# Top-k attention with a SwiGLU block on one core: K and Q through three rotating buffers, transposed one turn earlier, and exp moved to the head of the turn

## The chip, the cores and the metric

The kernel runs on one core of a Trainium2 chip, as one launch. The metric is the device time of that launch in microseconds (us); the kernel before takes 1888.62 us, the median of three runs that lie between 1886.95 and 1888.98 us. One more execution was taken with the hardware profiler; its span, from the first instruction to the last, is 1884.9 us.

The engines are named as the profile names them: PE is TensorE (its matmuls), PEld its weight loads, DVE is VectorE, ACT is ScalarE, POOL is GpSimd and SP is SyncE, which here only starts transfers. Each works through its own instructions in the order in which the program gives them.

## The reference, cut to what matters

Eight batches of eight heads, 576 positions, head size 64. Each query row keeps its 32 highest scores, takes the softmax of those, and weighs V. The result, 4608 rows of 512, goes through a SwiGLU block with 1536 hidden columns. All in float32.

```
scores = (q @ k.T) / sqrt(64)                       # 8 x 8 x 576 x 576
kth    = 32nd highest of each row
scores = where(scores >= kth, scores, -1e9)
attn   = exp(scores - max);  attn /= sum(attn) + 1e-9
x      = (attn @ v), heads side by side             # 4608 x 512
g      = x @ w_gate;  val = x @ w_val               # 512 x 1536 each
out    = (g * sigmoid(g) * val) @ w_out             # 1536 x 512
```

## The kernel before

**Units and turns.** Attention is cut into 160 units: batch b (8), query tile qt (5), pair of heads hp (4). 576 queries are four tiles of 128 rows and a rest of 64. A unit with qt = 0 to 3 has two heads of 128 rows ("two halves", 2 x 576 columns); in a unit with qt = 4 the two heads' last 64 rows lie on the two halves of the partitions, so that it has one stretch of 576 columns and half of the work on DVE. A turn n of the main loop holds DVE's selection for unit n (four rounds of MAX8 and MATCH_REPLACE, then a mask), and round it the other stages of units before and after it. So each batch has sixteen full turns and then four short ones. "The border" below means these four short turns and the turn that follows them, where one batch hands over to the next.

```
for n in range(NU + 4):                              # NU = 160
    nxt   = scores([n + 1, n + 2]) if n % 2 == 1 ...  # PE, ACT copies scores to sc
    ahead = fetch(n + 3)                             # transposes of K and Q, if that unit has qt == 0
    ...
    penalize(n - 1)                                  # POOL: e = mask + sc
    flush(on_pool); flush(on_act)                    # feed-forward work put off
    if n % 2 == 1 and n >= 5:
        finish_units([n - 5, n - 4])                 # PE: attn @ v, ACT copies to xT
    run(nxt)
    dve(2)                                           # DVE: steps of unit n's selection
    ...
    pieces(2); flush(on_act)                         # PE: feed-forward matmuls
    run(turn(n - 3))                                 # PE transposes e, ACT copies to et
    weigh(n - 1)                                     # ACT: exp of e, with the row sums
    dve(1); dve(1)
    run(norm)                                        # normalize(n - 2): DVE 1/sum, ACT e *= 1/sum
    next(ahead); pieces(1); run(ahead)
    dve(1); pieces(1); dve(2); run(topk); pieces(6)
```
(cut)

**Feed-forward work is handed out by credit.** `pieces(k)` issues up to k pieces (mostly four matmuls of 128x256) while `credit` lasts; each turn adds `share(n)`, which counts how much other PE work the turn has. What is left over at the end runs after the attention.

```
def share(n):
    others = 0.6
    if n % 2 == 1:
        for m in (n - 5, n - 4, n + 1, n + 2):
            if m >= 0:
                others += 0.3 if units[m][1] == J else 0.6
    if units[n + 3][1] == 0:
        others += 0.6
    beside = 6.4 if T[1] else 7.0
    return beside * n_heads(units[n][1]) / 2 - others
```

**K and Q.** For each of the 32 pairs of heads (batch, hp), `load` brings K and Q as one tile and their last 64 rows as another; `prep` turns them on PE and ACT copies them to a slab `kqT` (and the last keys to `klast`). From the second batch on, all pairs share one buffer of each kind.

```
kq      = ld.tile([P, 2, J, 2, D], ..., name="kq_in")      # ld: bufs=1
kq_last = ld.tile([P, 2, D], ..., name="kq_last")
for n, src in ((0, k), (1, q)):                            # four large and two small transfers on SP
    ...

def prep(i):
    for n, at in ((0, 0), (None, JP), (1, S)):             # K, last rows, Q
        ps = ps_t.tile([P, 512], FP32, tag="t")            # PSUM, 5 buffers shared by all attention stages
        ... PE transposes ...
        ... ACT copies to slab (last rows: also to klast) ...

def fetch(n):
    if qt == 0:
        yield from prep(i)
        if NHP <= i + 1 < len(pairs):
            load(i + 1)
```

**V.** `load_v` brings V as `vt` and V's last 64 rows twice: as `v_last` (64 rows, both heads beside each other) for the units with qt = 4, and as `vlast`, a 128x128 tile with one head in each diagonal block, for all others.

Of the kernel before, what the change touches and what calls it, by code (L numbers as in the profile page):

```python
# [11 lines left out]
FP32 = mybir.dt.float32  # L12
# [4 lines left out]
P = 128  # L17
# [11 lines left out]
def kernel(  # L29
# [57 lines left out]
    ld = ctx.enter_context(tc.tile_pool(name="ld", bufs=1))  # L87
    slabs = ctx.enter_context(tc.tile_pool(name="slabs", bufs=4))
# [3 lines left out]
    ffn = ctx.enter_context(tc.tile_pool(name="ffn", bufs=2))  # L92
# [134 lines left out]
    raw, preps = {}, {}  # L227
    HALVES = [slice(0, D), slice(D, P)]

    def load(i):  # L230
        b, hp = pairs[i]
        h = slice(2 * hp, 2 * hp + 2)

        if 1 <= i < NHP:
            kq = ffn.tile([P, 2, J, 2, D], FP32, tag="xT", name="kq_in", bufs=3)
            kq_last = ffn.tile([P, 4, 2, D], FP32, tag="h", name="kq_last", bufs=MS + 1)[:, 0]
        else:
            kq = ld.tile([P, 2, J, 2, D], FP32, tag="kq", name="kq_in")
            kq_last = ld.tile([P, 2, D], FP32, tag="kql", name="kq_last")[:]
        for n, src in ((0, k), (1, q)):  # L240
            for hh in range(2):
                queue = nc.scalar if hh == 1 and i == 0 else nc.sync
                queue.dma_start(  # L243
                    kq[:, n, :, hh, :],
                    src[b, 2 * hp + hh, 0:JP].rearrange("(p j) d -> p j d", j=J),
                )
            nc.sync.dma_start(
                kq_last[n * R : (n + 1) * R], src[b, h, JP:S].rearrange("h p d -> p h d")
            )
        raw[i] = (kq, kq_last)  # L250

    vs = {}

    def load_v(i):
        b, hp = pairs[i]
        h = slice(2 * hp, 2 * hp + 2)
        vt = slabs.tile([P, 2, J, D], FP32, tag="v", name="v")
        v_last = slabs.tile([R, 2, D], FP32, tag="vl", name="v_last")
        vl = vlast[hp]
        nc.sync.dma_start(  # L260
            vt[:].rearrange("p h j d -> p h (j d)"),
            v[b, h, 0:JP].rearrange("h (p j) d -> p h (j d)", j=J),
        )
        nc.sync.dma_start(v_last[:], v[b, h, JP:S].rearrange("h p d -> p h d"))
        for hh in range(2):
            o = hh * R
            nc.sync.dma_start(vl[o : o + R, o : o + R], v[b, 2 * hp + hh, JP:S])
        vs[i] = (vt, v_last, vl)

    def prep(i):  # L270

        kq, kq_last = raw.pop(i)
        slab = slabs.tile([P, JP + S], FP32, tag="kqT", name="kqT")
        for n, at in ((0, 0), (None, JP), (1, S)):
            ps = ps_t.tile([P, 512], FP32, tag="t", name="kqps")
            if n is None:
                nc.tensor.transpose(
                    ps[:, 0:P], kq_last.rearrange("p h d -> p (h d)"), ident[:]
                )
                for d in HALVES:  # L280
                    nc.scalar.copy(klast[pairs[i][1]][d, d], ps[d, 0:R])
                nc.scalar.copy(slab[:, at : at + R], ps[:, R:P])
                yield
                continue
            for c in range(J):
                nc.tensor.transpose(
                    ps[:, c * P : (c + 1) * P],
                    kq[:, n, c].rearrange("p h d -> p (h d)"),
                    ident[:],
                )  # L290
            nc.scalar.copy(slab[:, at : at + JP], ps[:])
        preps[i] = slab

    units = [(b, qt, hp) for b in range(B) for qt in range(J + 1) for hp in range(NHP)]
# [97 lines left out]
    def normalize(n):  # L392
        st = state[n]
        tot, e, heads = st.pop("tot"), st["e"], st.pop("heads")
        nh = len(heads)
        nc.vector.reciprocal(tot[:, 0:nh], tot[:, 0:nh])  # L396
        yield
        for t, hs in enumerate(heads):
            nc.scalar.mul(e[:, hs], e[:, hs], tot[:, t : t + 1])  # L399

    def turn(n):

        last = units[n][1] == J
        e = state[n].pop("e")
        et = work.tile([P, 2 * J + 1, P], FP32, tag="et", name="et")
        for c0, cn in ((0, J), (J, 1)) if last else ((0, J), (J, 1), (J + 1, J)):
            ps = ps_t.tile([P, 512], FP32, tag="t", name="etps")
            kl = R if last and c0 == J else P
            for c in range(cn):
                k0 = (c0 + c) * P  # L410
                nc.tensor.transpose(ps[0:kl, c * P : (c + 1) * P], e[:, k0 : k0 + kl], ident[:])  # L411
            nc.scalar.copy(  # L412
                et[0:kl, c0 : c0 + cn, :],
                ps[0:kl, 0 : cn * P].rearrange("p (c j) -> p c j", c=cn),
            )
            if c0 == J:
                yield
        state[n]["et"] = et
# [3 lines left out]
    def values(ns):  # L422

        b, qt, _ = units[ns[0]]
        last = qt == J
        ql = R if last else P
        ets = [state.pop(n)["et"] for n in ns]
        avs = [ps_t.tile([P, P], FP32, tag="t", name="av") for _ in ns]
        for n, et, av in zip(ns, ets, avs):
            vt, v_last, _ = vs[b * NHP + units[n][2]]  # L430
            for c in range(J + 1 if last else J):
                kl = R if c == J else P
                for hh in range(2):
                    moving = (
                        et[0:kl, c, hh * R : (hh + 1) * R]
                        if last
                        else et[:, c + hh * (J + 1), :]
                    )
                    nc.tensor.matmul(  # L439
                        av[hh * R : (hh + 1) * R, 0:ql],  # L440
                        v_last[:, hh, :] if c == J else vt[:, hh, c, :],
                        moving,
                        start=c == 0,
                        stop=last and c == J,
                    )
        for n, et, av in zip(ns, ets, avs):
            hp = units[n][2]
            vl = vs[b * NHP + hp][2]
            if not last:
                nc.tensor.matmul(av[:], vl[:], et[:, J, :], start=False, stop=True)  # L450
            c0 = b * S + qt * P
            at = c0
            while at < c0 + ql:
                kb = at // BLK
                n_c = min((kb + 1) * BLK, c0 + ql) - at
                if kb not in xT:
                    xT[kb] = ffn.tile([P, NHP, BLK], FP32, tag="xT", name="xT", bufs=3)
                    done[kb] = 0
                nc.scalar.copy(  # L459
                    xT[kb][:, hp, at - kb * BLK : at - kb * BLK + n_c],  # L460
                    av[:, at - c0 : at - c0 + n_c],
                )
                done[kb] += n_c
                at += n_c
# [227 lines left out]
    def fetch(n):  # L692

        b, qt, hp = units[n]
        i = b * NHP + hp
        if qt == 0:
            yield from prep(i)
            if NHP <= i + 1 < len(pairs):
                load(i + 1)

    def share(n):


        others = 0.6
        if n % 2 == 1:
            for m in (n - 5, n - 4, n + 1, n + 2):
                if m >= 0:
                    others += 0.3 if units[m][1] == J else 0.6
        if units[n + 3][1] == 0:
            others += 0.6  # L710

        beside = 6.4 if T[1] else 7.0
        return beside * n_heads(units[n][1]) / 2 - others

    def pieces(n):
        for _ in range(n):
            if credit[0] >= 1:
                credit[0] -= piece()

    def run(steps):  # L720
        for _ in steps:
            pass
# [5 lines left out]
            if qt == J and b + 1 < B:  # L728
                load_v((b + 1) * NHP + hp)

    load(0)
    rounding(2)
    load(1)
    run(fetch(0))
    run(scores([0]))
    run(fetch(1))
# [5 lines left out]
    for n in range(NU + 4):  # L742
# [34 lines left out]

        early[0]()
        run(nxt)

        dve(2, beside=False)
        if n == 0:
            load(2)
            load(3)
# [70 lines left out]
```

## Time and profile before

| what | value |
|---|---|
| time, median of 3 | 1888.62 us |
| span of the profiled execution | 1884.9 us |
| PE busy / granted clock over the span | 1709.4 us / 0.952 |
| DVE busy | 1624.2 us |
| ACT busy | 1195.5 us |
| POOL busy | 1014.3 us |
| a full turn on DVE where DVE waits for nothing | 10.56 us |
| a short turn on DVE where DVE hardly waits | 6.25 us |
| K or Q transfer, issue to landing | 2.9 and 3.0 us |

Busy time of an engine against the span tells which engine may set the end. The idle time of that engine, put down to what ended each wait, tells what could be won. The clock is the share of full speed that PE was granted: matmuls in a stretch at 0.5 take twice as long, and a busy PE hides that.

### The profile page before, as it was taken

What the parts mean: (1) busy time and instruction counts of PE and PEld (TensorE: products, weight loads), DVE (VectorE), ACT (ScalarE), POOL (GpSimd) and SP (SyncE); (2) the same over time, 40 slices, a digit from 0 to 9 for tenths busy, and PEclk for the clock granted to TensorE, in tenths of its full rate; (3) what the DMA queues carried; (4) which work ended last, traced back from release to release, by engine and by line L of the source; (5) the groups of instructions that cost most, each with busy time, mean ns of one, the idle gap of its engine ahead of it and who ended that gap; (6) DMA issues with size and microseconds to landing.
All of it is one profiled execution on the core that took longest, in us unless ns stands there. A gap on an engine that the chain in (4) does not pass through costs nothing.

```text
span 1884.9 us, 29941 instructions
## 1 busy us (share of the span) xinstructions
PE 1709.4 (91%) x10500; PEld 1389.6 (74%) x10500; DVE 1624.2 (86%) x3409; ACT 1195.5 (63%) x2847; POOL 1014.3 (54%) x932
## 2 busy tenths in 40 slices
PE   4447989899999989999999989999899999999998
PEld 2235758677788868787788867878788867788876
DVE  6999998999999989899999979898989989999400
ACT  5667666667666666667666675766676766576431
POOL 3555755645555636555456536555456644646434
PEclk7567999999999999999999999999999999999999
DMA  6333120001200030001210011000300011000000
GB/s 169 91 89 91 55 66 25 12 1 29 63 1 12 1 72 19 12 2 27 52 25 1 12 42 49 1 12 1 76 16 12 1 39 40 12 1 12 1 12 11
DMA packets 109142, 59.61 MB, mean 32 GB/s; under 512 B 88512, under 2 KB 96704, under 8 KB 108992
## 3 DMA queue, kind: packets, MB, share of 16 engines
q1 hardware_dynamic: 107936, 57.44, 11.7%
q8 instruction: 83, 1.36, 0.3%
q14 instruction: 67, 0.55, 0.1%
q10 hardware_dynamic: 1056, 0.26, 0.1%
HBM read 48.23 MB, written 9.44 MB: 31 GB/s over the span
## 4 chain that ended last, share of the span: by engine, by line
PE 70%; ACT 8%; POOL 5%; DVE 1%; SPq 1%; DMA 1%; issue 1%; POOLq 0%; ACTq 0%
PE f L504 36%; PE av L439 7%; PE x_ps L590 7%; PE s L332 6%; PE etps L411 5%; PE y_ps L590 4%; ACT e L384 2%; ACT e L399 2%; PE av L450 2%; ACT et L412 2%; PE last L315 1%; POOL p L576 1%; DMA kq_last<-in_q_dram 1%; POOL e L375 1%; SPq L243 1%
## 5 line engine op out<-in xcount | busy, mean ns | idle before, releaser
L375 POOL TENSOR_TENSOR e<-e,sc 128x1152 f32<-128x1152 f32 (+1 forms) x160 | 383.2, 2395 | 458.7 <-DVE e L363 344.3
L353 DVE MAX8 m<-e 128x8 f32<-128x576 f32 x864 | 612.8, 744 | 2.2
L357 DVE MATCH_REPLACE8 e<-m,e 128x576 f32<-128x576 f32 x576 | 423.1, 740 | 0.0
L504 PE MATMUL f<-xT,wg 128*128 128x256 f32 x1728 | 397.5, 381 | 1.4 <-ACT xT L459 1.4
L504 PE MATMUL f<-xT,wv 128*128 128x256 f32 x1728 | 396.3, 379 | 0.0
L504 PEld LDWEIGHTS f<-xT,wg 128*128 128x128 f32 x1728 | 324.8, 191 | 44.9 <-ACT xT L459 2.2
L504 PEld LDWEIGHTS f<-xT,wv 128*128 128x128 f32 x1728 | 322.5, 190 | 40.9
L384 ACT ACTIVATE e<-e,bias 128x576 f32<-128x576 f32 x288 | 224.8, 794 | 38.3 <-POOL e L375 38.3
L412 ACT COPY et<-etps 128x512 f32<-128x512 f32 (+1 forms) x448 | 183.7, 487 | 73.8 <-PE etps L411 73.4
L353 DVE MAX8 m<-sc 128x8 f32<-128x576 f32 x288 | 204.7, 746 | 28.7 <-ACT sc L338 25.1
L411 PE MATMUL etps<-ident,e 128*128 128x128 f32 (+1 forms) x1312 | 179.6, 282 | 47.9 <-ACT e L399 22.2
L439 PEld LDWEIGHTS av<-et,v 128*64 128x64 f32 x2560 | 139.1, 145 | 112.7 <-ACT sc L338 100.9
L399 ACT ACTIVATE e<-e,tot 128x576 f32<-128x576 f32 x288 | 207.0, 760 | 13.1 <-DVE tot L396 13.1
L357 DVE MATCH_REPLACE8 e<-m,sc 128x576 f32<-128x576 f32 x288 | 211.5, 740 | 0.0
L411 PEld LDWEIGHTS etps<-ident,e 128*128 128x128 f32 (+1 forms) x1312 | 156.8, 145 | 70.5 <-issue 36.5
L439 PE MATMUL av<-et,v 128*64 128x128 f32 (+1 forms) x2560 | 160.1, 280 | 45.1 <-ACT sc L338 45.1
L332 PE MATMUL s<-kqT 64*128 64x512 f32 (+1 forms) x640 | 182.0, 666 | 11.9 <-ACT et L412 6.6
L338 ACT COPY sc<-s 128x512 f32<-128x512 f32 x288 | 158.5, 604 | 49.2 <-PE s L332 49.2
L363 DVE TENSOR_SCALAR e<-sc,m 128x576 f32<-128x576 f32 x288 | 171.4, 631 | 1.1
L532 POOL TENSOR_TENSOR h<-h,half_g 128x512 f32<-128x512 f32 x108 | 139.3, 1290 | 43.9 <-ACT h L531 43.9
L537 POOL TENSOR_TENSOR h<-h,val 128x512 f32<-128x512 f32 x108 | 139.1, 1288 | 35.8 <-ACT val L536 31.9
L396 DVE RECIPROCAL tot<-tot 128x2 f32<-128x2 f32 (+1 forms) x160 | 25.1, 157 | 134.6 <-ACT tot L389 134.5
(74 smaller groups left out, 2055.0 us busy)
## 6 DMA issues: line engine op xcount, KB each, us to landing
v<-in_v_dram SPq DMA_DIRECT2D x32, 256.0 KB, 3.2
kq_in<-in_k_dram SPq DMA_DIRECT2D x63, 128.0 KB, 2.9
kq_in<-in_q_dram SPq DMA_DIRECT2D x63, 128.0 KB, 3.0
w<-in_moe_w_gate_dram SPq DMA_DIRECT2D x12, 512.0 KB, 3.9
w<-in_moe_w_val_dram SPq DMA_DIRECT2D x12, 512.0 KB, 3.8
w<-in_moe_w_out_dram SPq DMA_DIRECT2D x12, 512.0 KB, 3.5
out_dram<-o SPq DMA_DIRECT2D x40, 128.0 KB, 2.4
out_dram<-o SPq DMA_DIRECT2D x16, 256.0 KB, 2.4
```

The lines of the kernel that those rows point to most:

```text
L332: nc.tensor.matmul(ps, slab[d, queries], slab[d, 0:JP])
L353: nc.vector.max(m[:, t, 8 * r : 8 * r + 8], cur[:, hs])
L357: nc.vector.match_replace(e[:, hs], m[:, t, 8 * r : 8 * r + 8], cur[:, hs], LOWEST)
L363: nc.vector.tensor_scalar(e[:, hs], sc[:, hs], m[:, t, TOP_K - 1 : TOP_K], FAR, ALU.is_lt, ALU.mult)
L375: nc.gpsimd.tensor_tensor(e[:, every], e[:, every], sc[:, every], ALU.add)
L384: nc.scalar.activation(e[:, hs], e[:, hs], AF.Exp, bias=bias[:, t : t + 1], scale=scale, accum_out=tot[:, t : t + 1],)
L399: nc.scalar.mul(e[:, hs], e[:, hs], tot[:, t : t + 1])
L411: nc.tensor.transpose(ps[0:kl, c * P : (c + 1) * P], e[:, k0 : k0 + kl], ident[:])
L412: nc.scalar.copy(et[0:kl, c0 : c0 + cn, :], ps[0:kl, 0 : cn * P].rearrange("p (c j) -> p c j", c=cn),)
L439: nc.tensor.matmul(av[hh * R : (hh + 1) * R, 0:ql], v_last[:, hh, :] if c == J else vt[:, hh, c, :], moving, start=c == 0, stop=last and c ...
L504: nc.tensor.matmul(ps[:, i, :], w[:, kc, m * P : (m + 1) * P], x[:, kc, :], start=(kc == 0), stop=(kc == KC - 1),)
L590: nc.tensor.matmul(ps, lhsT, T[i][m], start=m == 0, stop=m == MQ - 1)
```

## The change

Four things are altered together.

1. K and Q of a pair become two tiles of their own kind, in three rotating buffers. When K of pair i has been transposed, Q of pair i+1 is loaded into its buffer; when Q of pair i has been transposed, K of pair i+2 takes that one. So K is loaded nearly two preparations ahead and Q one.
2. The transposes run one turn earlier: `fetch(n + 4)` takes the place of `fetch(n + 3)`, and `share` counts them there.
3. exp (`weigh`) moves from behind the transposes of e to the head of the turn, directly behind the copies of the scores.
4. V's last rows are kept once. For a unit with qt = 4, ACT copies the last 64 columns of e beside themselves, so that one transpose of 128 columns gives them on both halves of the partitions, and the product uses the diagonal blocks of `vlast`. The tile `v_last` and its 32 transfers go; its room pays for the third K/Q buffer.

The aim is that PE need not wait at the border for a transfer into the only K/Q buffer, nor for the copies of the slab that the next scores read.

```
-            kq = ld.tile([P, 2, J, 2, D], FP32, tag="kq", name="kq_in")
+            parts[what] = ld.tile([P, J, 2, D], FP32, tag="kq", name="kq_in", bufs=3)[:]
 ...
-        v_last = slabs.tile([R, 2, D], FP32, tag="vl", name="v_last")
-        nc.sync.dma_start(v_last[:], v[b, h, JP:S].rearrange("h p d -> p h d"))
 ...
     def prep(i):
+        ahead = NHP <= i and i + 1 < len(pairs)
         for what, at in ((0, 0), (2, JP), (1, S)):
             if what == 2:
 ...
+                if ahead:
+                    load(i + 1, 2)
                 yield
                 continue
 ...
             nc.scalar.copy(slab[:, at : at + JP], ps[:])
+            if ahead and what == 0:
+                load(i + 1, 1)
+            elif ahead and i + 2 < len(pairs):
+                load(i + 2, 0)
 ...
     def normalize(n):
         for t, hs in enumerate(heads):
             nc.scalar.mul(e[:, hs], e[:, hs], tot[:, t : t + 1])
+        if nh == 1:
+            nc.scalar.copy(e[:, S : S + R], e[:, JP:S])
 ...
-                nc.tensor.transpose(ps[0:kl, c * P : (c + 1) * P], e[:, k0 : k0 + kl], ident[:])
+                nc.tensor.transpose(ps[:, c * P : (c + 1) * P], e[:, k0 : k0 + P], ident[:])
 ...
-                        v_last[:, hh, :] if c == J else vt[:, hh, c, :],
+                        v_c, moving = vl[d, d], et[d, c, d]          # for c == J
 ...
-            if NHP <= i + 1 < len(pairs):
-                load(i + 1)
 ...
-        if units[n + 3][1] == 0:
+        if units[n + 4][1] == 0:
             others += 0.6
 ...
-            ahead = fetch(n + 3) if n + 3 < NU else no
+            ahead = fetch(n + 4) if n + 4 < NU else no
 ...
         run(nxt)
+        if 0 <= n - 1 < NU:
+            weigh(n - 1)
 ...
+        if n == 2 * NHP:
+            load_all(NHP)
+            load(NHP + 1, 0)
         pieces(2)
         flush(on_act)
         if 0 <= n - TURN < NU:
             run(turn(n - TURN))
-        if 0 <= n - 1 < NU:
-            weigh(n - 1)
```
(cut)

More of the change, by code (lines that the diff above doesn't have):

```diff
@@ L228, with load, load_all @@
     HALVES = [slice(0, D), slice(D, P)]
-    def load(i):
+    def load(i, what):
         b, hp = pairs[i]
         h = slice(2 * hp, 2 * hp + 2)
[L234 to L237, printed above, removed]
-            kq = ld.tile([P, 2, J, 2, D], FP32, tag="kq", name="kq_in")
[L239 to L245, printed above, removed]
-                )
-            nc.sync.dma_start(
-                kq_last[n * R : (n + 1) * R], src[b, h, JP:S].rearrange("h p d -> p h d")
-            )
-        raw[i] = (kq, kq_last)
+        parts = raw.setdefault(i, [None] * 3)
+        if what == 2:
+            if 1 <= i < NHP:
+                last = ffn.tile([P, 4, 2, D], FP32, tag="h", name="kq_last", bufs=MS + 1)
+                parts[2] = last[:, 0]
+            else:
+                parts[2] = ld.tile([P, 2, D], FP32, tag="kql", name="kq_last")[:]
+            for n, src in ((0, k), (1, q)):
+                nc.sync.dma_start(
+                    parts[2][n * R : (n + 1) * R], src[b, h, JP:S].rearrange("h p d -> p h d")
+                )
+            return
+        if not 1 <= i < NHP:
+            parts[what] = ld.tile([P, J, 2, D], FP32, tag="kq", name="kq_in", bufs=3)[:]
+        elif what == 0:
+            both = ffn.tile([P, 2, J, 2, D], FP32, tag="xT", name="kq_in", bufs=3)
+            parts[0], parts[1] = both[:, 0], both[:, 1]
+        for hh in range(2):
+            queue = nc.scalar if hh == 1 and i == 0 else nc.sync
+            queue.dma_start(
+                parts[what][:, :, hh, :],
+                (k, q)[what][b, 2 * hp + hh, 0:JP].rearrange("(p j) d -> p j d", j=J),
+            )
+    def load_all(i):
+        for what in (0, 2, 1):
+            load(i, what)
     vs = {}
@@ L267, in load_v @@
             nc.sync.dma_start(vl[o : o + R, o : o + R], v[b, 2 * hp + hh, JP:S])
-        vs[i] = (vt, v_last, vl)
+        vs[i] = (vt, vl)
     def prep(i):
-        kq, kq_last = raw.pop(i)
+        parts = raw.pop(i)
         slab = slabs.tile([P, JP + S], FP32, tag="kqT", name="kqT")
-        for n, at in ((0, 0), (None, JP), (1, S)):
+        ahead = NHP <= i and i + 1 < len(pairs)
+        for what, at in ((0, 0), (2, JP), (1, S)):
             ps = ps_t.tile([P, 512], FP32, tag="t", name="kqps")
-            if n is None:
+            if what == 2:
                 nc.tensor.transpose(
-                    ps[:, 0:P], kq_last.rearrange("p h d -> p (h d)"), ident[:]
+                    ps[:, 0:P], parts[2].rearrange("p h d -> p (h d)"), ident[:]
                 )
@@ L287, in prep @@
                     ps[:, c * P : (c + 1) * P],
-                    kq[:, n, c].rearrange("p h d -> p (h d)"),
+                    parts[what][:, c].rearrange("p h d -> p (h d)"),
                     ident[:],
@@ L407, in turn @@
             ps = ps_t.tile([P, 512], FP32, tag="t", name="etps")
-            kl = R if last and c0 == J else P
             for c in range(cn):
                 k0 = (c0 + c) * P
-                nc.tensor.transpose(ps[0:kl, c * P : (c + 1) * P], e[:, k0 : k0 + kl], ident[:])
+                nc.tensor.transpose(ps[:, c * P : (c + 1) * P], e[:, k0 : k0 + P], ident[:])
             nc.scalar.copy(
-                et[0:kl, c0 : c0 + cn, :],
-                ps[0:kl, 0 : cn * P].rearrange("p (c j) -> p c j", c=cn),
+                et[:, c0 : c0 + cn, :],
+                ps[:, 0 : cn * P].rearrange("p (c j) -> p c j", c=cn),
             )
@@ L429, in values @@
         for n, et, av in zip(ns, ets, avs):
-            vt, v_last, _ = vs[b * NHP + units[n][2]]
+            vt, vl = vs[b * NHP + units[n][2]]
             for c in range(J + 1 if last else J):
[L432 to L440, printed above, removed]
-                        v_last[:, hh, :] if c == J else vt[:, hh, c, :],
-                        moving,
-                        start=c == 0,
-                        stop=last and c == J,
+                for hh, d in enumerate(HALVES):
+                    if not last:
+                        v_c, moving = vt[:, hh, c, :], et[:, c + hh * (J + 1), :]
+                    elif c < J:
+                        v_c, moving = vt[:, hh, c, :], et[:, c, d]
+                    else:
+                        v_c, moving = vl[d, d], et[d, c, d]
+                    nc.tensor.matmul(
+                        av[d, 0:ql], v_c, moving, start=c == 0, stop=last and c == J
                     )
@@ L447, in values @@
             hp = units[n][2]
-            vl = vs[b * NHP + hp][2]
+            vl = vs[b * NHP + hp][1]
             if not last:
@@ L729, in finish_units @@
                 load_v((b + 1) * NHP + hp)
-    load(0)
+    load_all(0)
     rounding(2)
-    load(1)
+    load_all(1)
     run(fetch(0))
@@ L779 @@
         run(nxt)
+        if 0 <= n - 1 < NU:
+            weigh(n - 1)
         dve(2, beside=False)
         if n == 0:
-            load(2)
-            load(3)
+            load_all(2)
+            load_all(3)
         if n < NHP:
             load_v(n)
+        if n == 2 * NHP:
+            load_all(NHP)
+            load(NHP + 1, 0)
         pieces(2)
```

## The prediction

> **What bounds the kernel now.** I read the busy times first, then the same by stage, then PE's waits in the stage that counts, and last the timeline of one border.
>
> The page: busy time per engine, then busy tenths and clock in 40 slices of 47 us.
> ```profile
> PE 1709.4 (91%) x10500; PEld 1389.6 (74%) x10500; DVE 1624.2 (86%) x3409; ACT 1195.5 (63%) x2847; POOL 1014.3 (54%) x932
> ...
> PE   4447989899999989999999989999899999999998
> DVE  6999998999999989899999979898989989999400
> PEclk7567999999999999999999999999999999999999
> ```
> PE and DVE are both near full, but not in the same place. DVE is full from the second slice and falls to nothing in the last two, where PE still works off feed-forward pieces. Busy time by stage makes it plain (columns: length, busy us and instructions of PE, PEld, DVE, ACT, POOL, granted clock, DMA share, GB/s):
> ```profile
> 0.00:205.00 205.00, 112.25 (x534) 80.29 (x535) 186.09 (x394) 125.80 (x278) 108.34 (x101) 0.71 0.39 108
> 205.00:385.00 180.00, 163.32 (x980) 122.76 (x978) 168.25 (x349) 120.19 (x289) 105.46 (x92) 0.95 0.12 33
> 385.00:1740.00 1355.00, 1301.62 (x8255) 1073.69 (x8256) 1246.63 (x2625) 899.24 (x2175) 737.80 (x672) 0.99 0.09 22
> 1740.00:1885.00 145.00, 132.20 (x734) 112.88 (x733) 23.22 (x44) 50.32 (x109) 62.70 (x68) 0.97 0.03 8
> ```
> Up to 205 us DVE bounds: PE idles 93 us there, and a saved PE wait is worth nothing. From 205 to 385 the two alternate. From 385 to 1740 DVE idles 108 us and PE 53 us (1355 - 1302): PE's in-order chain bounds, since the left-over pieces follow it without a gap. I take every PE wait in this stage as worth its length, plus what it costs in clock; DVE's 108 us are the room for it. PE's waits in this stage (total, times, longest; smaller ones left out):
> ```profile
> PE av L439 <- ACT sc L338: 10.7, 4, 3.3
> PE last L315 <- ACT kqT L291: 9.9, 6, 3.0
> PE x_ps L590 <- POOL h L638: 7.1, 7, 2.7
> PE kqps L277 <- DMA kq_last<-in_q_dram: 7.0, 7, 1.2
> PE kqps L286 <- DMA kq_in<-in_k_dram: 6.6, 5, 1.6
> PE kqps L286 <- ACT et L412: 3.2, 5, 1.5
> ```
> Three kinds concern the change: the first product of the next batch waiting for its slab (9.9), the K/Q transposes waiting for transfers (7.0 + 6.6 + 0.3 = 13.9) and the same transposes waiting for ACT, which has the PSUM buffers or the queue (3.2, and with the smaller rows 9.5). Together 33.3 of 53 us, all at borders.
>
> The clock at two borders against the batch: busy time by window again.
> ```profile
> 666.00:697.00 31.00, 24.46 (x148) 18.40 (x148) 24.93 (x54) 22.42 (x60) 9.47 (x10) 0.89 0.34 80
> 883.00:914.00 31.00, 26.45 (x160) 20.60 (x160) 27.61 (x58) 23.07 (x62) 9.96 (x10) 0.89 0.29 66
> ```
> Not only does PE idle 5 to 6 us there, it also has 0.89 of its clock. Six such windows (453 to 480 up to 1532 to 1566; clocks 1.00, 0.89, 0.89, 0.94, 0.94, 0.90) lose 0 + 3.4 + 3.4 + 1.9 + 1.7 + 3.4 = 13.8 us against full clock. One border in the timeline (start, length, engine, what, idle before):
> ```profile
> 677.86 0.59 ACT L291 COPY kqT<-kqps 128x512 f32<-128x512 f32 x1
> ...
> 678.50 0.79 PE L315 MATMUL last<-klast,kqT 128*128 128x128 f32 x2 [3.04 <-ACT kqT L291]
> ...
> 679.23 3.79 PE L332 MATMUL s<-kqT 64*128 64x512 f32 x8
> ...
> 682.02 1.42 DVE L353 MAX8 m<-sc 128x8 f32<-128x576 f32 x2 [2.69 <-ACT sc L338]
> ```
> ACT ends the slab, PE waited 3.04 us for it, and then eight score matmuls take 3.79 us; at full clock they take 1.99 us (at 553). Even DVE waits 2.69 us for what comes out.
>
> **What the Trainium skill says.** "TensorE: Matmul & The Clock Gate", Part 1: PE has two clocks, and an idle window of about 3.4 us drops it to half until a busy one follows. The trace agrees: the score matmuls after 3.04 us of idle take 3.79 instead of 1.99 us. The same page, Part 1, on queue depths: ScalarE and VectorE are strict first-in-first-out. That makes exp at the turn's head risky, and the trace agrees: at 767 ACT stood 5.63 us before exp for the mask addition on POOL, with the scores' copies behind it. "DMA: Bandwidth & Descriptors", Rules for kernel authors: issue early, wait late. A transfer lands 2.9 to 3.0 us after issue here, and a short turn is 6.25 us, so one preparation ahead should hide it.
>
> **The change part by part**, in us of the end time.
>
> *K and Q in three buffers.* Before, all six transfers of a pair start when the buffer is free, about 5.3 us of issue time on SP (0.62 to 1.30 per row), and the last of them lands just as its transpose wants it. After, K is there a turn early, and Q and the last rows are issued first after the K transposes. Of 13.9 I take off 10; a store waiting on POOL in the same queue may hold up the rest.
>
> *One turn earlier.* The slab is ready a turn before its scores, so the 9.9 go but for 1 at PSUM buffers: -9. PE's own work does not change: nine transposes per pair, moved. But all four preparations now fall into the four short turns, where before the fourth fell into the next full turn. Each brings ACT 2 x 0.58 + 3 x 0.21 = 1.8 us, and ACT is already busy 22.4 of 31 us there. So the 9.5 of waits for ACT stay and grow: +2.
>
> *Clock.* With about 19 of 33 us of idle gone, I take back 8 of the 13.8: the deepest gaps (3.04) go, the other sparse stretches stay. -8.
>
> *exp at the head.* The same 288 exps of 0.79 us, no new work. I took for each unit the end of the ACT instruction that will stand before its exp, and the end of the mask addition it needs. In the PE-bound stage some nine in ten are ready long before (DVE runs 9 to 16 us ahead), and exp fills a hole in which ACT waited for PE. In the others, ACT will stand. The worst are five units (65, 73, 109, 145, 153) where POOL sums up a feed-forward block first: 8.1 us of standing in place of 4.3 to 5.6. It ends at the same instant, but the copies of et (1.24) now come after exp instead of before, so the scores' copies and PE's av come later: three of them have PE gaps of 3.1 to 3.3 today, each longer by some 1.5: +4.5. In the DVE-bound stage the same standing costs nothing.
>
> *V's last rows.* 32 transfers less, hidden anyway. 32 copies of 128x64 more on ACT: estimate 0.21 each from the slab's 128x64 copies (213 ns), 6.8 in all, a quarter of it on the path: +1.5. The transpose of 128 instead of 64 columns streams the same 128 columns: 0.
>
> Sum: -10 - 9 + 2 - 8 + 4.5 + 1.5 = **-19**, so 1888.6 - 19 = 1869.6, and I say 1869.
>
> **The rivals.** *Everything at the borders goes*: all 33.3 of idle and 13.8 of clock, 47 in all, 1842. For it: DVE has room (it idles 6.1 and 3.4 us in the two windows shown). Against: PSUM's five shared buffers and ACT stay. *ACT becomes the bound in the short turns*: the idle is only renamed from transfers and slab to ACT, the clock stays low, and exp's standing adds: 1885 to 1890. For it: my count of ACT work in four short turns is 31 us (exp, normalizing, copies of et, scores, slabs and pieces) against 25 of DVE and 26 of PE. Against: at these borders ACT still idles over 8 us in 31, waiting for the very PE that waits. *exp at the head stalls ACT in the batch*, so copies of feed-forward products come late and PE waits there: up to 10 more than my sum, 1880. *The start*: exp waits for POOL in the DVE-bound stage too; if DVE's rounding steps are held up by it, some us more.
>
> **Range and chances.** The first rival bounds it below, the second above; both need a full reversal of something I see. 8 in 10: 1850 to 1887. Faster by over 2% means under about 1851: 0.12. Slower by over 2% would need a stall in every turn: 0.03. Within 2%: 0.85.
>
> **What would show it.** In the profile after: no "last" waiting for kqT and at most 4 us of K/Q transfers in PE's waits (right: buffers and turn); mean clock in the border windows 0.94 or more (right: clock); kqps waiting for ACT around 10 to 13 us, and if over 20, the second rival; exp waiting for POOL above 50 us in total against 38.3 now, with av waiting for sc around 15 against 10.7. Up to 205 us nothing should differ by more than 2 us. What would make it wrong: a shift of feed-forward blocks against the units, which moves the five coincidences, or DVE bounding at the borders once PE is quick.

## The result, and the profile after

The changed kernel takes **1860.18 us** (median of four, 1859.1 to 1862.81). The kernel before took 1887.78 us in the four runs that it is compared with: a ratio of **0.9857**, 95% interval 0.984 to 0.9874, so 27.6 us or 1.4% less. A second set gave 1860.49 us and 0.9854 (0.9829 to 0.9878). The profiled span fell from 1884.9 to 1858.6 us.

Busy time per engine and PE's busy tenths in 40 slices of the span, from the page of the changed kernel:
```profile
PE 1713.0 (92%) x10500; PEld 1394.9 (75%) x10500; DVE 1641.1 (88%) x3409; ACT 1197.0 (64%) x2879; POOL 1015.3 (55%) x932
...
PE   4467889989999999999999999999999999999998
```
No engine does less: PE has the same 10500 instructions, ACT 32 more. What went is PE's idle time (1858.6 - 1713.0 = 145.6 us against 175.5). By stage, in the columns of the prediction's second view (length; busy us and instructions of PE, PEld, DVE, ACT, POOL; clock, DMA share, GB/s), the last line being the border that was shown of before at 666:
```profile
0.00:205.00 205.00, 116.37 (x525) 81.14 (x526) 184.88 (x391) 124.58 (x276) 108.65 (x101) 0.70 0.38 109
205.00:385.00 180.00, 165.43 (x988) 124.49 (x987) 174.78 (x353) 120.80 (x294) 105.95 (x92) 0.95 0.12 32
385.00:1715.00 1330.00, 1299.48 (x8252) 1076.37 (x8251) 1263.21 (x2631) 900.76 (x2200) 738.01 (x672) 0.99 0.09 22
1715.00:1859.00 144.00, 131.73 (x739) 112.88 (x738) 18.23 (x38) 50.81 (x112) 62.65 (x67) 0.97 0.04 8
655.00:686.00 31.00, 27.92 (x208) 21.24 (x208) 24.92 (x53) 24.58 (x67) 12.09 (x13) 1.00 0.36 83
```
The gain lies in the third line: the stage holds as many PE instructions as before (8252 against 8255) in 1330 instead of 1355 us, with 30.5 us of PE idle (1330 - 1299.48) instead of 53.4. The border at 655 has 208 matmuls in 31 us where there were 148, at full clock instead of 0.89. Nothing is gained at the start or in the tail.

PE's waits in that stage of the changed kernel (total, times, longest; us; one of 0.4 left out):
```profile
PE s L350 <- ACT et L432: 13.2, 5, 2.8
PE kqps L299 <- ACT et L432: 9.4, 11, 1.1
PE x_ps L606 <- POOL h L654: 3.0, 2, 1.7
PE s L350 <- ACT kqT L304: 2.6, 6, 0.6
PE av L459 <- ACT sc L356: 0.7, 1, 0.7
```
Both lines that the change aimed at are gone: transfers (13.9 us before) and "last" waiting for its slab (9.9). What is left of the slab is 2.6 us of score matmuls waiting for PSUM buffers. A new line leads the list: score matmuls waiting for the copies of et, 13.2 us in five waits. It stands where "av waiting for sc" stood with 10.7.

### The profile page after: what moved, and what is told of

Same layout as the page of the kernel before. It is cut to its first block, busy times and chain, and to the rows that moved or that the text cites. A ratio compares the mean times of both kernels' runs of the same rounds, so it can differ in the third digit from the quotient of the medians.

```text
span 1858.6 us, 29975 instructions
## 1 busy us (share of the span) xinstructions
PE 1713.0 (92%) x10500; PEld 1394.9 (75%) x10500; DVE 1641.1 (88%) x3409; ACT 1197.0 (64%) x2879; POOL 1015.3 (55%) x932
## 4 chain that ended last, share of the span: by engine, by line
PE 68%; ACT 10%; POOL 6%; DVE 2%; issue 1%; POOLq 0%; ACTq 0%
PE f L520 37%; PE av L459 7%; PE s L350 7%; PE x_ps L606 5%; PE etps L431 5%; PE y_ps L606 3%; ACT e L402 3%; POOL e L393 2%; ACT et L432 2%; PE av L466 2%; ACT e L417 2%; POOL p L592 1%; ACT sc L356 1%; PE last L333 1%; POOL h L654 1%; DVE m L371 1%
## 5 line engine op out<-in xcount | busy, mean ns | idle before, releaser
L402 ACT ACTIVATE e<-e,bias 128x576 f32<-128x576 f32 x288 | 224.5, 793 | 96.3 <-POOL e L393 96.3
L350 PE MATMUL s<-kqT 64*128 64x512 f32 (+1 forms) x640 | 197.5, 665 | 50.8 <-ACT et L432 41.1
L431 PE MATMUL etps<-ident,e 128*128 128x128 f32 x1312 | 178.9, 281 | 45.2 <-ACT e L417 21.8
L417 ACT ACTIVATE e<-e,tot 128x576 f32<-128x576 f32 x288 | 212.9, 794 | 5.6 <-DVE tot L414 5.6
L431 PEld LDWEIGHTS etps<-ident,e 128*128 128x128 f32 x1312 | 157.4, 145 | 67.8 <-issue 32.8
L432 ACT COPY et<-etps 128x512 f32<-128x512 f32 (+1 forms) x448 | 182.3, 480 | 17.1 <-PE etps L431 17.1
L381 DVE TENSOR_SCALAR e<-sc,m 128x576 f32<-128x576 f32 x288 | 189.3, 693 | 1.1
L354 ACT COPY sc<-last 128x128 f32<-128x128 f32 (+1 forms) x160 | 42.5, 266 | 185.0 <-PE last L333 157.8
```

Source lines behind the costliest of these rows:

```text
L350: nc.tensor.matmul(ps, slab[d, queries], slab[d, 0:JP])
L381: nc.vector.tensor_scalar(e[:, hs], sc[:, hs], m[:, t, TOP_K - 1 : TOP_K], FAR, ALU.is_lt, ALU.mult)
L402: nc.scalar.activation(e[:, hs], e[:, hs], AF.Exp, bias=bias[:, t : t + 1], scale=scale, accum_out=tot[:, t : t + 1],)
L431: nc.tensor.transpose(ps[:, c * P : (c + 1) * P], e[:, k0 : k0 + P], ident[:])
L432: nc.scalar.copy(et[:, c0 : c0 + cn, :], ps[:, 0 : cn * P].rearrange("p (c j) -> p c j", c=cn),)
```

## The experiments

The kernel before varied by some 10 us within one set of runs (1885.69 to 1895.84), so each run is compared with the kernel before on its own chip, by ratio. Two quantities from the profiles go with the times, both over the stage from 385 to 1740 us or nearly so: PE's waits, and *clock lost*, which is the length of each clock record from 400 to 1740 us times what it lacks to full clock (before 17.1 us, after 6.8). Both come from the one profiled execution of each kernel, and the clock lost differs between executions: after_again, the same kernel as after, has 10.2.

| kernel | us | ratio | 95% interval | clock lost, us |
|---|---|---|---|---|
| after | 1860.18 | 0.9857 | 0.984 to 0.9874 | 6.8 |
| exp_middle | 1869.72 | 0.9893 | 0.9865 to 0.9921 | 8.5 |
| exp_alone | 1885.32 | 0.9974 | 0.996 to 0.9987 | 17.1 |
| turn_alone | 1872.88 | 0.991 | 0.9882 to 0.9939 | 11.9 |
| v_alone | 1875.62 | 0.993 | 0.991 to 0.995 | 10.2 |
| turn_later | 1873.36 | 0.9906 | 0.988 to 0.9932 | 23.9 |
| two_buffers | 1866.61 | 0.9871 | 0.9848 to 0.9894 | 15.4 |
| turn_and_exp | 1868.71 | 0.9889 | 0.9861 to 0.9917 | 15.4 |
| exp_deferred | 1836.88 | 0.9715 | 0.9692 to 0.9737 | 3.4 |
| v_dead_load | 1876.24 | 0.9931 | 0.991 to 0.9951 | 18.8 |
| buffers_and_v | 1868.48 | 0.9896 | 0.9871 to 0.9922 | 17.1 |
| after_again | 1860.49 | 0.9854 | 0.9829 to 0.9878 | 10.2 |
| exp_middle_again | 1869.62 | 0.9899 | 0.9874 to 0.9923 | 8.5 |

### exp_middle: the changed kernel with exp back behind the transposes of e

```
         run(nxt)
-        if 0 <= n - 1 < NU:
-            weigh(n - 1)
 ...
             run(turn(n - TURN))
+        if 0 <= n - 1 < NU:
+            weigh(n - 1)
```


> The changed kernel with one part undone: exp goes back behind the transposes of e, in the middle of the turn; buffers, earlier turn and V's rows stay. Theory (the transfers and the slab at the borders were the cost, exp at the head only adds standing where POOL sums up a block): the border waits stay gone, the waits of the score matmuls for the copies of et (13.2 us between 385 and 1715) go, those of av for the scores' copies come back (about 10 us); the time stays within 8 us of the changed kernel's 1860, rather below it, 1852 to 1862. Rival (exp at the head does the work, because ACT then ends the turn early and the slab's copies come sooner): the waits of kqps for ACT grow from 9.4 to 20 or more and the time goes back to 1872 or above.

It is 9.5 us slower than the changed kernel, where the prediction's sum has exp at the head as a loss of 4.5. Waits of PE:
```profile
PE av L459 <- ACT sc L356: 14.2, 4, 4.8
PE s L350 <- ACT kqT L304: 13.4, 10, 2.2
PE x_ps L606 <- POOL h L654: 7.1, 7, 2.7
PE kqps L299 <- ACT et L432: 2.7, 3, 0.9
...
PE kqps L288 <- ACT et L432: 1.1, 1, 1.1
```
The first line is the price that the prediction put on exp; moving exp turns 14.2 into 13.2 + 0.7, which is about even. The gain is in the next two: 13.4 becomes 2.6 and 7.1 becomes 3.0. In the second line, the score matmuls wait for PSUM buffers that still hold turned K and Q, because ACT does exp and the normalizing before it copies the slab. With exp at the head, ACT comes to the slab earlier: after 400 us its large copies start 3.0 us on average behind the last of their transposes in exp_middle, and 2.4 in the changed kernel. Part of the gain is paid back in the last two lines: the K/Q transposes wait 3.8 us for ACT here, and 9.4 with exp at the head.

### exp_alone: the kernel before with exp at the head

```
         run(nxt)
+        if 0 <= n - 1 < NU:
+            weigh(n - 1)
 ...
-        if 0 <= n - 1 < NU:
-            weigh(n - 1)
         dve(1); dve(1)
```


> The kernel before with exp moved to the turn's head and nothing else. Theory: the border waits for transfers (13.9 us) and for the slab (9.9) stay as they were or nearly, standing of ACT for the mask addition grows from 38 to about 90 us; time 1885 to 1895. Rival (exp at the head does the work): the slab's copies come sooner, the wait of the first product falls below 4 us, and the time is 1875 or below.

A small gain, not a loss: 0.9974 (0.996 to 0.9987). Here the five coincidences do cost more (13.1 + 0.7 instead of 10.7), and the waits for transfers grow (13.9 to 15.5), but "last" waiting for the slab falls from 9.9 to 6.1, and the feed-forward products waiting for POOL from 7.1 to 2.5. Exp at the head therefore has a price, and two benefits that outweigh it.

### turn_alone: the kernel before with its transposes one turn earlier

```
-        if units[n + 3][1] == 0:
+        if units[n + 4][1] == 0:
 ...
-            ahead = fetch(n + 3) if n + 3 < NU else no
+            ahead = fetch(n + 4) if n + 4 < NU else no
```


> The kernel before with the K/Q transposes one turn earlier (and the credit counted there), still one pair's buffer and exp in the middle. Theory: the wait of the first product for its slab (9.9 us) goes with its clock loss, the waits for transfers (13.9 us) stay or grow, because all four preparations are now in short turns: 1872 to 1882. Rival (the turn alone does everything, buffers are for nothing): 1863 or below, with waits for transfers under 5 us.

1872.88 us, ratio 0.991. "last" no longer waits for the slab and the transfers cost 7.3 instead of 13.9 us. But a wait that was not there has come:
```profile
PE s L332 <- ACT kqT L291: 11.6, 9, 2.2
```
It is the same PSUM wait as in exp_middle: with exp in the middle, the wait for the slab is not so much removed as passed on to the next matmul. The transposes' own waits for ACT fall from 9.5 to 2.6 us.

### turn_later: the changed kernel with its transposes where they were

It is turn_alone's edit undone in the changed kernel: `fetch(n + 3)`, and `share` counts `units[n + 3]`.

> The changed kernel with the K/Q transposes (and their credit) back to one turn later; three buffers, exp at the head and V's single rows stay. If the earlier turn is worth what it gave alone (16 us), the time is about 1876 and the first product waits for its slab again, 6 to 12 us between 385 and 1740; waits for K/Q transfers stay near zero. If the buffers alone already free the border (the slab is copied early enough because its transposes no longer wait), the time is 1866 or below with the slab's wait under 4 us.

It loses 13.2 us of the 27.6 (some 9 by the ratios, 0.9906 against 0.9857). PE's first waits, and busy time in the window of the same border (columns as above):
```profile
PE s L350 <- ACT et L432: 13.2, 5, 2.8
PE last L333 <- ACT kqT L304: 12.0, 7, 2.2
```
```profile
655.00:686.00 31.00, 26.65 (x184) 19.63 (x183) 22.95 (x48) 23.48 (x63) 9.30 (x12) 0.89 0.27 65
```
Transfers cost 0.2 us in all, without the earlier turn, so that is the buffers' doing; the slab and the clock are the turn's. Where 12.0 us of idle stay at the borders, the clock goes to 0.89 again (0.94 at the next border).

### v_alone: the kernel before with V's last rows kept once

Part 4 of the change alone; `load` and `prep` as before. The edits to V, `normalize`, `turn` and `finish_units` are those of the diff above.

> The kernel before with V's last rows kept once (32 transfers less, 32 ACT copies of 128x64 more). Theory: 32 copies of some 0.2 us, mostly beside other work: 1888 to 1892, no faster. Rival (fewer transfers in the queue of SP free the K/Q loads): waits for K/Q transfers fall by half or more and the time is below 1883.

13.6 us faster (0.993), where the prediction had +1.5. The waits for K/Q transfers fall from 13.9 to 6.5 us, although nothing was done to K and Q:
```profile
PE last L313 <- ACT kqT L289: 12.5, 6, 3.3
...
PE kqps L284 <- DMA kq_in<-in_k_dram: 4.7, 4, 1.8
...
PE kqps L275 <- DMA kq_last<-in_q_dram: 1.4, 2, 0.9
...
PE kqps L284 <- DMA kq_in<-in_q_dram: 0.4, 1, 0.4
```
SP's timeline shows what has changed for them (start, length of issuing, what). First the kernel before, at a border:
```profile
685.82 2.41 SPq L267 DMA_DIRECT2D vlast<-in_v_dram  x4
688.34 0.62 SPq L247 DMA_DIRECT2D kq_last<-in_k_dram  x1
689.07 1.25 SPq L243 DMA_DIRECT2D kq_in<-in_k_dram  x2
```
and v_alone at the same place:
```profile
685.72 0.62 SPq L247 DMA_DIRECT2D kq_last<-in_k_dram  x1
...
701.00 2.09 SPq L265 DMA_DIRECT2D vlast<-in_v_dram  x2
```
Before, the tile `vlast` is free early, as the short units do not use it, so its small transfers are started between the K/Q transfers, which stand behind them in SP's queue by 2.41 us. With V's rows kept once, `vlast` is in use until the short units are done, and its transfers go behind. But not all of the 13.6 us is in these waits: the slab's has grown from 9.9 to 12.5, and PE's waits from 385 to 1740 us in all fall by 5.6 (52.9 to 47.3). For the rest no single wait can be named.

### v_dead_load: v_alone with the 32 transfers back

```
+        v_last = slabs.tile([R, 2, D], FP32, tag="vl", name="v_last")
+        nc.sync.dma_start(v_last[:], v[b, h, JP:S].rearrange("h p d -> p h d"))
```
The tile is loaded and read by nothing.

> The kernel before with V's last rows used from the one tile only, but the second tile still loaded and read by nothing: the 32 transfers are back, the order of the queue stays that of the run with V alone (the diagonal blocks' transfers behind V's, not among those of K and Q, because their tile is now in use until the short units are done). If their place in the queue was the cost: about 1876 as with V alone, waits for K/Q transfers 5 to 8 us between 385 and 1740. If the number of transfers was: 1885 or above and 12 us or more.

1876.24 us, the same as v_alone: the number of transfers costs nothing that could be measured. That leaves their place in the queue, which the timeline shows; no run changes that place alone. The K/Q transfers cost 4.5 us here. The clock lost (18.8 us against 10.2) belongs to the two profiled executions, which also differ in time (1879.85 and 1873.06 us); the medians don't.

### buffers_and_v: the changed kernel with both exp and the transposes where they were

> The changed kernel with exp back in the middle and the transposes back to one turn later, so that only the three buffers and V's single rows are left. Theory: waits for K/Q transfers are gone, the wait of the first product for its slab stays at 10 to 16 us between 385 and 1740, time 1872 to 1878, little below V alone (1875.6). If the buffers were the main part: 1867 or below.

1868.48 us. The transfers are fully hidden (no such line is left), and in exchange PE waits longer for the slab:
```profile
PE last L333 <- ACT kqT L304: 18.8, 7, 3.3
```
Against v_alone, the third buffer brings 7.1 us; in the two traces 4.0 of it lie in the first 400 us (PE's 1600th matmul starts at 395.4 instead of 399.4). With this run the two moves can be crossed, with buffers and V in place. The median time, and the profiled execution split where PE's 1600th matmul starts, all in us:

| transposes | exp | median | to the 1600th matmul | from there to the last |
|---|---|---|---|---|
| late | in the middle (buffers_and_v) | 1868.5 | 395.4 | 1463.6 |
| early | in the middle (exp_middle) | 1869.7 | 403.9 | 1457.2 |
| late | at the head (turn_later) | 1873.4 | 396.8 | 1467.1 |
| early | at the head (after) | 1860.2 | 400.6 | 1450.3 |

**In the whole time neither move gains anything alone here; both together gain 8.** The split shows what hides in this: the earlier turn loses 8.5 us in the start and gains 6.4 behind it, while exp at the head alone gains in neither. Both together gain 13.3 behind the start, so the moves do need each other. (after_again and exp_middle_again give 1451.8 and 1457.3.) At about 240 us PE has one wait of 5.98 us in exp_middle and of 5.35 in the changed kernel, against 2.96 in turn_later; that this is the loss in the start is likely, but not shown. Without buffers and V the same two moves add up: ratios 0.991 and 0.9974 alone, 0.9889 together.

### two_buffers: the changed kernel with two K/Q buffers

```
-            parts[what] = ld.tile(..., name="kq_in", bufs=3)[:]
+            parts[what] = ld.tile(..., name="kq_in", bufs=2)[:]
 ...
-            if ahead and what == 0:
-                load(i + 1, 1)
-            elif ahead and i + 2 < len(pairs):
-                load(i + 2, 0)
+            if ahead and what == 1:
+                load(i + 1, 0)
+                load(i + 1, 1)
```
K and Q of the next pair are loaded only when Q of this one has been turned.

> The changed kernel with two K/Q buffers instead of three: K and Q of the next pair are both loaded only when Q of this pair has been transposed; earlier turn, exp at the head and V's single rows stay. If the third buffer takes the transfers off PE's path: waits for K/Q transfers of 5 to 10 us between 385 and 1720, each renewing the clock loss, time 1866 to 1872. If removing V's second load (20 us less queue work) already did that: waits under 3 us and time within 3 us of 1860.

1866.61 us, 6.4 more than the changed kernel; by ratio 0.9871 against 0.9857, with intervals that overlap. The trace has one wait of note that the changed kernel hasn't, and more clock lost (15.4 us against 6.8 and 10.2 in the two executions of that one): Q's transpose waits 3.5 us for Q's transfer, in two waits. So the third buffer seems worth a few us, once V is out of the way and the transposes are earlier; the ratios don't tell it from nothing.

### turn_and_exp: the kernel before with both moves and nothing else

> The kernel before with the earlier turn and exp at the head, no third buffer and V's rows still loaded twice. If the parts simply add (16.3 and 3.9 us): 1869. If exp at the head is worth more once the turn is earlier (score matmuls wait 11.6 us for PSUM buffers that the slab's copies free, and exp at the head lets these copies come sooner, as between the run with exp in the middle and the changed kernel, 9.5 us): 1862 to 1866 and that wait under 4 us.

1868.71 us, what the simple sum gave. The wait for PSUM buffers did fall, from 11.6 to 2.6 us, but the transposes' waits for ACT rose from 2.6 to 9.1. From here V and two buffers of the new kind lead to two_buffers, only 2.1 us lower, although V alone had brought 13.6. Both the earlier turn and V take away the same waits for transfers. Of 16.3 (turn), 13.6 (V), 3.9 (exp) and 7.1 (buffers over V), in all 40.9 us, the change as a whole keeps 27.6.

### after_again and exp_middle_again: the sign of exp's term once more

The changed kernel and exp_middle, unaltered, on one chip.

> The changed kernel once more, unaltered, beside the next run on the same chip, because the sign of the exp term rests on a difference of some 9 us between runs of different chips, and the intervals of the two ratios nearly touch. If exp at the head gains: ratio to the kernel before 0.985 to 0.987, and 5 to 10 us below the run with exp in the middle.

> The changed kernel with exp in the middle of the turn, once more, beside the unaltered one. If exp at the head gains: 1867 to 1871, ratio 0.989 to 0.991, intervals apart. If the difference came from the chips: within 3 us of the unaltered one.

1860.49 against 1869.62: exp at the head is worth 9.1 us beside the other parts. The clock lost, 10.2 and 8.5 us, does not account for it; PE's waits from 385 to 1740 us do (29.3 and 40.1).

### exp_deferred: exp at the head, except where POOL is late

```
 def sum_up(...):                 # POOL sums up a feed-forward block
+    summed[0] = True
 ...
         penalize(n - 1)
+        late.append(n - 1)
+        hold = n % 2 == 0 and summed[0]
+        summed[0] = False
 ...
         run(nxt)
-        if 0 <= n - 1 < NU:
-            weigh(n - 1)
+        while late and not hold:
+            weigh(late.pop(0))
```
In the eight even turns that follow such a sum, exp is put off to the head of the next turn. The computation is unchanged.

> The changed kernel with one addition: in the even turns where POOL has summed up a feed-forward block just before (8 of 160), exp is not put at the head but put off to behind the scores' copies of the next turn, so that ACT does not stand for the mask addition with the copies of et behind it. If that standing is what the waits of the score matmuls for et cost (13.2 us between 385 and 1715, with the clock loss after each, 6.8 us): the waits fall below 4 us and the time to 1842 to 1852. If DVE is held up instead by the late row sums (it may then lead by half a turn only): waits of DVE for the sums grow by 10 us or more and the time is 1858 or above.

**1836.88 us**, ratio 0.9715 (0.9692 to 0.9737): 23.3 us below the changed kernel (some 27 by the ratios), below both kernels and below the 1842 to 1852 that were expected. One coincidence in the timeline of the changed kernel (start, length, engine, what, idle before; rows of ACT and PE):
```profile
758.86 0.78 ACT L402 ACTIVATE e<-e,bias 128x576 f32<-128x576 f32 x1 [8.13 <-POOL e L393]
...
760.97 1.24 ACT L432 COPY et<-etps 128x512 f32<-128x512 f32 x3
...
761.61 3.78 PE L350 MATMUL s<-kqT 64*128 64x512 f32 x6 [2.54 <-ACT et L432]
...
765.32 3.46 PE L459 MATMUL av<-et,v 128*64 128x128 f32 x32
...
769.26 1.03 PE L520 MATMUL f<-xT,wg 128*128 128x256 f32 x4
```
and in exp_deferred:
```profile
753.59 1.24 ACT L432 COPY et<-etps 128x512 f32<-128x512 f32 x3 [1.36 <-PE etps L431]
...
758.36 1.99 PE L350 MATMUL s<-kqT 64*128 64x512 f32 x8
...
760.28 1.97 PE L459 MATMUL av<-et,v 128*64 128x128 f32 x32
...
762.72 3.62 PE L521 MATMUL f<-xT,wg 128*128 128x256 f32 x16
...
764.25 0.82 ACT L402 ACTIVATE e<-e,bias 128x576 f32<-128x576 f32 x1
```
In the first, ACT stands 8.13 us with the copies of et behind it. PE's score matmuls wait 2.54 us for the PSUM buffers, and then six of them take 3.78 us and the 32 products with V 3.46 us, against 1.99 for eight and 1.97 for 32: PE runs at half speed after the gap. The next feed-forward matmuls start at 769.26 instead of 762.72 us, 6.5 us for one gap of 2.54. In exp_deferred's list of PE's waits the line of score matmuls waiting for et is gone; it begins with these two, and what follows is 2.1 us in all:
```profile
PE kqps L299 <- ACT et L432: 10.4, 7, 2.8
PE x_ps L607 <- POOL h L656: 3.0, 2, 1.7
```
PE is idle 131.1 us (1836.0 - 1704.9) against 145.6, and busy 1704.9 against 1713.0: 14.5 us less of idle, and 8.1 less for the same 10500 instructions, as fewer of them run at half speed.

## Why the prediction was right, and where its steps were not

The time, 1869 with a range of 1850 to 1887, was 9 us high and held, in part by luck: two terms have the wrong sign. Beside the other parts exp at the head brings 9.1 us where +4.5 stood, and V alone 13.6 where +1.5 stood; the sum survived because the parts overlap. Its terms, with the changes that the two traces show:

| step | predicted | measured |
|---|---|---|
| K and Q in three buffers | -10 | transfers 13.9 to 0: -13.9 |
| one turn earlier | -9 | slab 9.9 to 0, PSUM wait of 2.6 new: -7.3 |
| ACT in the short turns | +2 | transposes waiting for ACT 9.5 to 9.4: 0 (2.6 with the earlier turn alone) |
| clock | -8 | PE busy for the same work (411 to 1571 us before, 414 to 1545 after) 1111.8 to 1105.8: -6.0 |
| exp at the head | +4.5 | 10.7 to 13.2 + 0.7: +3.2; products waiting for POOL 7.1 to 3.0: -4.1 |
| V's last rows | +1.5 | part of the first row: with V alone 13.9 to 6.5 |

These make -28.1. With a small wait that went (1.4, feed-forward products for a copy of x) and 2.7 lost at the start (below), that is -26.8, where the profiled span fell by 26.3.

**Buffers and turn: right, but not whose gain it was.** "No last waiting for kqT and at most 4 us of transfers" came true: 0 and 0. But each part has a claim to the 13.9: V alone takes 7.4 of it, the earlier turn alone 6.6, and the buffers on top of V the rest. I had written that of six transfers the last lands just in time; that the queue ahead of them was held up by `vlast` I had not looked at. It was even in my figure: at the border that I showed, the six rows of a pair take 3.8 us of issuing on SP (0.62 + 1.25 + 1.30 + 0.63), and 5.3 only together with the row of `vlast` ahead of them.

**V: wrong.** The failed step is "32 transfers less, hidden anyway" with +1.5. V alone brings 13.6 us. v_dead_load shows that the 32 transfers indeed cost nothing. What is left is that the other tile, `vlast`, stays in use and its transfers no longer stand ahead of K's; the traces show this, but only part of the 13.6 us can be read from PE's waits. As this also shortens waits that I had given to the buffers, the sum suffered less than the term.

**exp at the head: the standing right, the sign wrong.** ACT stands 8.13 us where I worked out 8.1; exp waits 96.3 us for POOL in the whole run (I said over 50, against 38.3), and the five waits are longer by 3.2 us in place of 4.5. They have moved, though: not av waiting for sc, where I said 15, but the score matmuls before it, waiting for et's PSUM buffers. What I left out is what an earlier exp sets free behind itself. I had counted only what stands behind exp at its new place, not what no longer stands behind it at its old one: the slab's copies (exp_middle 13.4, after 2.6) and the feed-forward products that wait for POOL (7.1, after 3.0), against 5.6 more for the transposes that wait for ACT. The wait for POOL falls in every run with exp at the head and in none without; by what route, the runs don't tell.

**Clock: right in kind.** All six border windows have 1.00 (I asked for 0.94). PE's busy time for the same work falls by 6.0 us (1105.8 in after_again too). The Trainium skill, "TensorE: Matmul & The Clock Gate", Part 1, puts the drop to half clock behind an idle window of about 3.4 us. Here shorter gaps are enough: half speed follows PE gaps of 3.04 us (before, at 678) and 2.54 us (after, at 761). exp_deferred shows it best, 1.97 against 3.46 us for the same 32 matmuls. A small misreading: in the two windows that I showed, PE idles 6.5 and 4.6 us, not "5 to 6".

**The rivals.** "ACT becomes the bound in the short turns" did not happen: the transposes wait 9.4 us for ACT, just below my 10 to 13, and with the 2.6 of PSUM 12.0 in all. But my reason for the +2 failed: with the earlier turn alone ACT's queue delays the transposes less (2.6) and the score matmuls instead (11.6), and it is exp at the head that brings the 9.4 back. "Everything at the borders goes", 1842, went a good part of the way: transfers and slab are gone, ACT's share is not. "exp stalls ACT in the batch" is what remains in the changed kernel, and it is the largest item, though net of it exp still gains; exp_deferred takes it away. At the start, DVE's busy time up to 205 us differs by 1.2 us, within my 2; the same PE work is done at 414 us instead of 411, a loss of 2.7 us that I had not counted. It goes with the earlier turn (the table under buffers_and_v); why, the runs don't show.

## What to carry to other kernels

On an engine that works strictly in order, price a move at both ends: what it puts behind the operation, and what it releases from behind its old place. Waits that end at the same border hide one another, so the worth of a part must be measured with the others in place: here the parts, three measured alone and the buffers on top of V, came to 40.9 us and together to 27.6. Where an operation waits for a slow engine only in some turns, put it off in those turns alone; a gap of 2.5 us on PE cost 6.5 us with its clock.

## What was not expected of the hardware

POOL can hold up DVE's masks. DVE's masks in the kernel before, and two of the changed kernel's in its timeline (durations in ns: least, median, most; then start, length, engine, what):
```profile
L363 DVE TENSOR_SCALAR e<-sc,m x288: 490/511/2877, 28.1 to 1784.5; 128x576 f32<-128x576 f32 x144
```
```profile
550.74 2.64 POOL L393 TENSOR_TENSOR e<-e,sc 128x1152 f32<-128x1152 f32 x1
550.80 3.80 DVE L381 TENSOR_SCALAR e<-sc,m 128x576 f32<-128x576 f32 x2
```
A mask takes 0.51 us, but these two take 3.80: they start 0.06 us after POOL's addition, and the first of them (2.90 us) ends 0.3 us after that has ended. All 71 masks of the changed kernel that take over 0.6 us overlap an instruction of POOL, ten of them this addition; of the 217 others 48 do. MAX8 of the same size shows none of it (730 to 762 ns). This agrees with the Trainium skill, "SBUF — State Buffer", Who interferes with whom: a tensor_scalar can, if its operands allow it, take the port pair that DVE and GpSimd share, the pair is locked for a whole instruction, and the one that comes second stands still. The 288 masks take 189.3 us in the changed kernel and 171.4 before; at 0.51 us each they would take 147. The 17.9 us between the two kernels are all of DVE's 16.9 us more of busy time (1641.1 against 1624.2). It comes with exp at the head: 183.3 to 191.3 us in every kernel that has it, 166.4 to 171.4 in every other. Whether part of it can be had back in the first 205 us, where DVE bounds, no run tried.
